# Seven up-projections and four down-projection groups, one to a slot, inside a band attention that two MLPs follow

## The chip, the cores and the metric

The kernel runs on one core of a Trainium2 chip. The metric is the device time of one execution in microseconds. A core has five engines with instruction queues of their own: TensorE (PE in the rows; PEld is its weight load), VectorE (DVE), ScalarE (ACT), GpSimd (POOL) and SyncE (SP, which here issues nearly all DMAs). They work in parallel and wait for each other through semaphores; each takes its own instructions in order.

## The reference, cut to what matters

```python
def _attn_ref(q_l, k_l, v_l, q_g, k_g, v_g):      # B=4, H=8, 512 local + 32 global rows, D=64
    s_g = scale * q_g @ k_all.T;  out_g = softmax(s_g) @ v_all         # global rows see all keys
    s_ll = where(abs(i - j) <= 32, scale * q_l @ k_l.T, -1e9)          # local rows: a band
    s_lg = scale * q_l @ k_g.T                                         # and the global keys
    out_l = softmax(concat([s_lg, s_ll])) @ concat([v_g, v_l])
    return concat([out_g, out_l], axis=2)

x = attention(...)                                 # 2304 tokens x 512
h = x @ w_in;   x = elu(h) @ w_out                 # first MLP, 512 -> 2048 -> 512
h = x2 @ w_in2; y = clipped_square(h) @ w_out2     # second MLP: ((h+1)^2/4 between -1 and 1)
```

All of it is float32.

## The kernel before, in words

**The MLPs.** The tokens stand in columns: four blocks of 512 (j = 0 to 3, one for each batch element) and one of 128 global rows (GR). An *up-projection* (class `Up`, f, j) makes 128 of the 2048 hidden features of one block: every float32 operand is split into a high and a low part, so it takes 12 matmuls of 512 columns (3 products x 4 slices), then `curve` (two ScalarE activations), `join` (VectorE), `high` (ScalarE, `gh`) and `low` (VectorE, `gl`). `down` multiplies the hidden tiles of a chunk of weights into four output tiles (d = 0 to 3), 3 matmuls for each f and d, and `collect` copies or adds the sum into `acc`. The first chunk holds f = 0 to 2, the second f = 3 to 6. The MLPs are written in plain loops, and a scheduler sets the order of the instructions on every engine; `later` puts the down matmuls three steps behind the ups.

**Weights** come as float32 pairs of words (64-bit rows, `wraw`) and are decoded by `prep` (line 160) into a high part `wh` and a low part `wl`, for a tile of 128 x 1024: an `Abs` on ScalarE, five VectorE operations, a copy to `wh` on ScalarE, and two more VectorE operations of which the last makes `wl`. In the attention a tile is decoded in two halves of 512 columns (six parts: three of up weights, then three of down weights).

**The attention** is a pipeline of 24 units, in groups of three: local rows of a pair of heads, global rows of four heads, local rows of the next pair. In slot n (the loop at line 722) unit n is at its scores (`s` or `sg`, `top`, `expo`), unit n-1 at its transposes and values (`pt` or `tg`, `po` or `pog`), unit n-2 at its norm, its transposes back (`ot`, or `tg3`, which the rows call `tg`) and the split into `xh` and `xl`. All calls inside the attention go through `Pinned`: each engine runs them in exactly the order written. Block j of the MLP is complete in x when slot 6j + 7 is through.

**Loads** stand in SP's queue in the order that `arrive` calls them: q and k of a pair, its two v halves, and the raw weight parts. `load` adds a limit: a load waits until so many older ones have landed that no more than 2700 words a partition are in flight (q 544, k 576, a v half 1040, a raw part 1024). q and k have two buffers each, v four, raw weights one.

**The dense work inside the attention** before: `early_ups` (line 672) makes five up-projections, and is stepped twice a slot from slot 10: four matmuls in the first slot of a group, eight in the second, then the curve, the join, the high and the low part each half a slot later. `early_weights` (line 665) steps a part's decode once a slot from slot 4. At the end, in slot 24, two of the four down tiles of block 0 are made (line 746). What is left of the five goes after the loop.

## Time and profile before

| | |
|---|---|
| median of 3 runs | 874.63 us (870.61 to 876.02) |
| profiled execution | 871.58 us, span 869.8 us |
| mean granted TensorE clock | 0.994 |
| busy: TensorE / VectorE / ScalarE / GpSimd | 851.5 / 584.3 / 431.2 / 47.5 us |
| attention, to the first free down matmul | 0 to 140.78 us |
| the MLPs | from there to the end |

The span is one execution as the hardware profiler saw it on the core; the time of the run beside it is longer by what lies around the span. A row of the timeline gives the start of an instruction (or of several alike in a row, "x64"), its duration, the engine, the line, the operation and its tiles, and in brackets how long the engine had idled and what ended that. Since matmuls are pipelined, the pace is read from start to start, not from the duration. Line 111 is that of `Pinned`, so every attention instruction has it and is told apart by its tile.

### The profile page before, as it was taken

To read this page: it belongs to the slowest core of one execution; us is meant where nothing else is said; L and a number is where in the kernel's file an instruction comes from. 1 tells how busy PE (TensorE), PEld (TensorE's weight loads), DVE (VectorE), ACT (ScalarE), POOL (GpSimd) and SP (SyncE) were. 2 spreads that over 40 slices of the span, in tenths; PEclk is the share of its full clock that TensorE was granted. 3 is DMA by queue.
4 is the path that set the end of the run, shared out by engine and by line. 5 is a ranking of instruction groups with operands and counts; after the bars stand their busy time and mean duration, and the time that the engine had idled before them with its cause. 6 is when DMAs were issued, how large, how long until landed. Compare 5 with 4: busy or idle time off the path is not lost.

```text
span 869.8 us, 14560 instructions
## 1 busy us (share of the span) xinstructions
PE 851.5 (98%) x5946; PEld 698.5 (80%) x5946; DVE 584.3 (67%) x1130; ACT 431.2 (50%) x755; POOL 47.5 (5%) x98
## 2 busy tenths in 40 slices
PE   8889999999999999999999999999999999999998
PEld 5666778888888888888888888888888888888886
DVE  5788874877635873833389897368859754845455
ACT  5677864766434543534256564456435433433332
POOL 4234220000000000000000000000000000000000
PEclk9999999999999999999999999999999999999999
DMA  7777751231200220110012112002201200000014
GB/s 262 252 233 232 227 174 54 101 133 55 97 1 1 96 97 1 49 49 1 1 49 96 49 50 97 0 2 98 96 0 49 97 1 1 0 1 1 2 58 148
DMA packets 19027, 65.43 MB, mean 75 GB/s; under 512 B 3984, under 2 KB 4240, under 8 KB 15248
## 3 DMA queue, kind: packets, MB, share of 16 engines
q1 hardware_dynamic: 18672, 64.23, 21.7%
q8 instruction: 47, 0.77, 0.3%
q10 hardware_dynamic: 288, 0.26, 0.1%
q14 instruction: 20, 0.16, 0.1%
HBM read 60.03 MB, written 4.46 MB: 74 GB/s over the span
## 4 chain that ended last, share of the span: by engine, by line
PE 92%; DMA 5%; ACT 1%; DVE 1%; issue 0%; POOL 0%; SPq 0%; POOLq 0%
PE dn L318 40%; PE up L245 39%; DMA v_sb<-in_vwin 4%; PE up L242 3%; PE dn L335 3%; PE s L111 2%; PE pt L111 1%; PE po L111 1%; PE up L111 1%; PE pog L111 1%; PE sg L111 1%; DMA k_sb<-in_kT 1%; ACT sn L111 1%; PE tg L111 1%; PE idle L111 1%; PE dn L111 1%
## 5 line engine op out<-in xcount | busy, mean ns | idle before, releaser
L318 PE MATMUL dn<-gh,wh 128*128 128x512 f32 x506 | 196.9, 389 | 0.0
L318 PE MATMUL dn<-gl,wh 128*128 128x512 f32 x506 | 196.8, 389 | 0.0
L318 PE MATMUL dn<-gh,wl 128*128 128x512 f32 x506 | 196.3, 390 | 0.0
L245 PE MATMUL up<-xh,wl 128*128 128x512 f32 x492 | 192.4, 391 | 0.0
L245 PE MATMUL up<-xl,wh 128*128 128x512 f32 x492 | 191.6, 390 | 0.0
L245 PE MATMUL up<-xh,wh 128*128 128x512 f32 x492 | 191.6, 389 | 0.0
L276 ACT ACTIVATE gh<-g 128x512 fp32r<-128x512 f32 x123 | 77.7, 632 | 119.1 <-DVE g L265 71.9
L295 DVE TENSOR_TENSOR acc<-dn,acc 128x512 f32<-128x512 f32 x128 | 84.8, 685 | 48.5 <-PE dn L318 48.3
L318 PEld LDWEIGHTS dn<-gl,wh 128*128 128x128 f32 x506 | 95.0, 188 | 19.8
L280 DVE TENSOR_TENSOR gl<-g,gh 128x512 fp32r<-128x512 f32 x123 | 84.6, 689 | 38.8 <-ACT gh L276 37.8
L318 PEld LDWEIGHTS dn<-gh,wh 128*128 128x128 f32 x506 | 95.0, 188 | 19.5
L318 PEld LDWEIGHTS dn<-gh,wl 128*128 128x128 f32 x506 | 95.0, 188 | 19.4
L245 PEld LDWEIGHTS up<-xh,wh 128*128 128x128 f32 x492 | 92.3, 188 | 19.2
L245 PEld LDWEIGHTS up<-xl,wh 128*128 128x128 f32 x492 | 92.4, 188 | 18.9
L245 PEld LDWEIGHTS up<-xh,wl 128*128 128x128 f32 x492 | 92.4, 188 | 18.8
L256 ACT ACTIVATE g<-up,half_sb 128x512 f32<-128x512 f32 (+1 forms) x69 | 46.9, 680 | 113.9 <-PE up L245 105.1
L264 DVE SCALAR_TENSOR_TENSOR g<-g 128x512 f32<-128x512 f32 (+1 forms) x69 | 46.9, 680 | 59.5 <-ACT g L256 59.4
L262 DVE SCALAR_TENSOR_TENSOR g<-up,g 128x512 f32<-128x512 f32 x64 | 43.4, 679 | 62.8 <-ACT g L253 62.8
L251 ACT ACTIVATE g<-up 128x512 f32<-128x512 f32 x64 | 37.8, 590 | 85.9 <-PE up L245 80.3
L265 DVE TENSOR_TENSOR g<-g,e 128x512 f32<-128x512 f32 (+1 forms) x69 | 47.0, 681 | 3.6
L178 ACT ACTIVATE top<-wraw 128x1024 f32<-128x1024 f32 x29 | 33.6, 1160 | 28.9 <-DMA wraw<-in_w 22.8
L253 ACT ACTIVATE g<-g,one_sb 128x512 f32<-128x512 f32 x64 | 45.9, 717 | 1.8
(112 smaller groups left out, 956.9 us busy)
## 6 DMA issues: line engine op xcount, KB each, us to landing
wraw<-in_w SPq DMA_DIRECT2D x29, 1024.0 KB, 4.8
v_sb<-in_vwin SPq DMA_DIRECT2D x32, 520.0 KB, 4.5
k_sb<-in_kT SPq DMA_DIRECT2D x16, 288.0 KB, 4.0
q_sb<-in_qT SPq DMA_DIRECT2D x16, 272.0 KB, 4.4
outT<-acc SPq DMA_DIRECT2D x16, 256.0 KB, 2.1
wraw<-in_w SPq DMA_DIRECT2D x6, 512.0 KB, 4.4
outT<-acc_rows SPq DMA_DIRECT2D x4, 64.0 KB, 2.2
mask_sb<-in_mask ACTq DMA_DIRECT2D x1, 192.0 KB, 4.0
```

The lines of the kernel that those rows point to most:

```text
L111: return lambda *args, **kw: tc.keep_in_program_order(fn(*args, **kw))
L245: eng.tensor.matmul(self.ps, w, x, start=k == 0, stop=k == 3 * KT - 1)
L251: eng.scalar.activation(self.g, self.ps, AF.Exp)
L253: eng.scalar.activation(self.g, self.g, AF.Relu, bias=one_sb, scale=-1.0)
L256: eng.scalar.activation(self.g, self.ps, AF.Relu, bias=half_sb, scale=0.5)
L262: eng.vector.scalar_tensor_tensor(g, self.ps, 0.0, g, ALU.max, ALU.subtract)
L264: eng.vector.scalar_tensor_tensor(g, g, 1.0, g, ALU.min, ALU.mult)
L265: eng.vector.tensor_tensor(g, g, self.e, ALU.add)
L276: eng.scalar.activation(self.gh, self.g, AF.Copy)
L280: eng.vector.tensor_tensor(self.gl, self.g, self.gh.bitcast(F32), ALU.subtract)
L295: eng.vector.tensor_tensor(a, ps, a, ALU.add)
L318: eng.tensor.matmul(banks[d], w[:, d * P:(d + 1) * P], g, start=f == fs[0] and k == 0, stop=f == fs[-1] and k == 2,)
```

## The change

- Inside the attention the tables `UPS` and `DOWNS` name what slot does what: an up-projection (f, j) with all its 12 matmuls in slots 8, 11, 14, 15, 16, 17 and 24, a down tile (j, d) of the first chunk with its 9 matmuls in slots 20 to 23. They stand behind the transposes and before the values of the slot. The curve follows in the same slot; join, high and low come in the next.
- The sums of block 0 are so complete; the two tiles made in slot 24 are of block 1. `sums` notes what the MLP's loop leaves out.
- A raw weight part is requested at the head of `arrive` in slots 3, 6, 9, 11, 13 and 15, and its decode begins two slots later: `Abs`, then a stage with `wh`, then a stage with `wl`, a slot each. Raw, `top` and `power` have two buffers in the attention.
- The decode: `wh` is rounded from the whole number, and `wl` is what that leaves plus the last bits, which come from a 16-bit word. Seven VectorE operations as before, one tensor_scalar less and one two-input operation more.
- `acc` of blocks 0 and 1 is set up before slot 20 in memory that the decode leaves; `gh` and `gl` have six buffers in place of five; the diagonal blocks for the global queries are one tile, and their zeros feed the warm-up.

```diff
-UP_EARLY = 5
 
 BANKS = (2, 3, 1)
 
-PREP_AT = 4
-UP_AT = 9
-
-UP_STEP = 4
+PREP_FROM = (3, 6, 9, 11, 13, 15)
+
+UPS = {8: (0, 0), 11: (1, 0), 14: (2, 0), 15: (0, 1), 16: (1, 1), 17: (2, 1), 24: (0, 2)}
+DOWNS = {20: (0, 0), 21: (0, 1), 22: (0, 2), 23: (0, 3)}
...
-    h_p = ctx.enter_context(tc.tile_pool(name="h", bufs=LAG + 2))
+    h_p = ctx.enter_context(tc.tile_pool(name="h", bufs=LAG + 3))
     ps_up = [ctx.enter_context(tc.tile_pool(name="ps_up", bufs=1, space=PSUM))]
     ps_dn = []
+    e_p = []
...
-    def prep(wraw_p, wtmp_p, layer, f, c0, n, raw_tag="wraw"):
+    def prep(wraw_p, wtmp_p, layer, f, c0, n, bufs=1):
...
-        raw = wraw_p.tile([P, n], U64, tag=raw_tag, name="wraw")
+        raw = wraw_p.tile([P, n], U64, tag="wraw", name="wraw", bufs=bufs)
         load(raw, (w1, w2)[layer][f][:, c0:c0 + n], 2 * n)
-        words = raw.bitcast(U32).rearrange("p (n two) -> p n two", two=2)
-        low, high = words[:, :, 0], words[:, :, 1]
-        top = wtmp_p.tile([P, n], U32, tag="top", name="top")
-        power = wtmp_p.tile([P, n], U32, tag="power", name="power")
-        rest = wtmp_p.tile([P, n], U32, tag="rest", name="rest")
+        high = raw.bitcast(U32).rearrange("p (n two) -> p n two", two=2)[:, :, 1]
+        low = raw.bitcast(U16).rearrange("p (n four) -> p n four", four=4)[:, :, 1]
         yield
 
+        top = wtmp_p.tile([P, n], U32, tag="top", name="top", bufs=bufs)
         eng.scalar.activation(top.bitcast(F32), high.bitcast(F32), AF.Abs)
-        eng.vector.tensor_scalar(rest, high, 0x1FF, 15, ALU.bitwise_and, ALU.logical_shift_left)
-        eng.vector.scalar_tensor_tensor(
-            rest, low, 17, rest, ALU.logical_shift_right, ALU.bitwise_or
-        )
         yield
-
         eng.vector.tensor_scalar(
             top.bitcast(F32), top.bitcast(F32), SMALLEST, 1.0, ALU.max, ALU.mult
         )
 
-        eng.vector.tensor_scalar(top, top, 3, 0x3FFFF000, ALU.logical_shift_left, ALU.bitwise_and)
+        eng.vector.tensor_scalar(top, top, 3, 0x3FFFFFF8, ALU.logical_shift_left, ALU.bitwise_and)
         eng.vector.scalar_tensor_tensor(
             top, high, 0xC0000000, top, ALU.bitwise_and, ALU.bitwise_or
         )
+        eng.scalar.activation(hi, top.bitcast(F32), AF.Copy)
+        power = wtmp_p.tile([P, n], U32, tag="power", name="power")
+        eng.vector.tensor_scalar(power, top, 0xFF800000, None, ALU.bitwise_and)
         yield
-        eng.scalar.activation(hi, top.bitcast(F32), AF.Copy)
-        eng.vector.tensor_scalar(power, top, 0xFF800000, None, ALU.bitwise_and)
-        eng.vector.scalar_tensor_tensor(
-            lo, rest, 2.0 ** -35, power.bitcast(F32), ALU.mult, ALU.mult
-        )
+
+        rest, number = power.bitcast(F32), top.bitcast(F32)
+        eng.vector.scalar_tensor_tensor(rest, low, 2.0 ** -36, rest, ALU.mult, ALU.mult)
+        eng.vector.tensor_tensor(number, number, hi.bitcast(F32), ALU.subtract)
+        eng.vector.tensor_tensor(lo, number, rest, ALU.add)
...
-        early = count[0] < UP_EARLY or count[0] % 4 == 0
-        count[0] += 1
+        early = len(ps_up) == 1 or count[0] % 4 == 0
+        count[0] += len(ps_up) > 1
...
-        def early_weights():
-
-            for part in parts:
-                for _ in range(3):
-                    next(part, None)
-                    yield
-
-        def early_ups():
-
-            for f, j in [(f, j) for j in range(B) for f in chunks[0][1]][:UP_EARLY]:
-                u = Up(0, f, j)
-                u.products(UP_STEP)
-                yield
-                yield
-                u.products(3 * KT - UP_STEP)
-                yield
-                u.curve()
-                yield
-                u.join()
-                yield
-                u.high()
-                yield
-                u.low()
-
-        parts = [prep(g_p, wtmp_p, 0, *part, raw_tag="wraw") for part in halves]
-        sent = iter(parts)
-        weights, ups = early_weights(), early_ups()
+        def early_down(j, d):
+
+            bank = up_bank()
+            fs = chunks[0][1]
+            for f in fs:
+                wh, wl = (w[:, KT * P:] for w in wtiles[0, f])
+                gh, gl = made[0, f, j]
+                for k, (w, g) in enumerate(((wl, gh), (wh, gh), (wh, gl))):
+                    eng.tensor.matmul(
+                        bank, w[:, d * P:(d + 1) * P], g,
+                        start=f == fs[0] and k == 0, stop=f == fs[-1] and k == 2,
+                    )
+            collect(0, fs, j, d, bank)
+            sums.add((j, d))
+
+        parts = [prep(early_wraw_p, wtmp_p, 0, *part, bufs=2) for part in halves]
+
+        def request(n):
+
+            if n in PREP_FROM:
+                next(parts[PREP_FROM.index(n)])
+
+        def prepare(n):
+
+            for i in range(4, 1, -1):
+                if n - i in PREP_FROM:
+                    next(parts[PREP_FROM.index(n - i)], None)
...
+            request(n)
...
-                next(next(sent, iter([0])))
-                if more:
...
+        u = None
         for n in range(len(units) + 2):
-            if n > UP_AT:
-                next(ups, None)
             part(n, "scores")
             part(n - 2, "norm")
+            if u:
+                u.join()
             part(n - 1, "turn")
             part(n - 1, "copy")
             part(n - 2, "back")
             part(n, "top")
             part(n - 2, "low")
             part(n, "expo")
-            if n >= PREP_AT:
-                next(weights, None)
-            if n >= UP_AT:
-                next(ups, None)
+            prepare(n)
+            if u:
+                u.high()
+                u.low()
+                u = None
+            if n in UPS:
+                u = Up(0, *UPS[n])
+                u.products(3 * KT)
+                u.curve()
+            elif n in DOWNS:
+                early_down(*DOWNS[n])
             part(n - 1, "values")
-
             arrive(n)
+            if n == min(DOWNS) - 1:
+
+                prep_ctx.close()
+                pool = mpool("acc_early", 1)
+                for j in range(2):
+                    acc[j] = pool.tile([P, KT, SL], F32, name=f"acc{j}")
             if n == len(units):
 
                 s_ctx.close()
                 ps_dn.append(mpool("ps_dn0", 1, space=PSUM))
                 for f in chunks[0][1]:
-                    down(0, chunks[0][1], 0, f, made[0, f, 0], first, range(KT // 2))
-        for _ in weights:
-            pass
-        for _ in ups:
-            pass
-        prep_ctx.close()
+                    down(0, chunks[0][1], 1, f, made[0, f, 1], first, range(KT // 2))
+                sums.update((1, d) for d in range(KT // 2))
         eng = free
 
     pool = mpool("acc", 1)
-    for j in range(1, B):
+    for j in range(2, B):
         acc[j] = pool.tile([P, KT, SL], F32, name=f"acc{j}")
     acc[GR] = pool.tile([P, KT * P], F32, name="acc_rows")
+    e_p.append(mpool("e", 1, side="right"))
...
-                    banks = {} if ci + j else first
+                    banks = first if (ci, j) == (0, 1) else {}
                 if (layer, f, j) not in made:
                     up(layer, f, j)
-                ds = range(KT) if ci + j else range(KT // 2, KT)
+                ds = [d for d in range(KT) if ci or (j, d) not in sums]
```

On **VectorE**, from the end of slot 9 (the `xl` of a global unit) to the reductions of slot 10; `den` to `o_sb` is the norm of the local unit 8. Before:

```order
L111 TENSOR_TENSOR xl_84<-tg_1111,xh_79 128x2x32
L111 TENSOR_SCALAR power<-top 128x512
L111 SCALAR_TENSOR_TENSOR wl_89<-rest,power 128x512
L111 TENSOR_SCALAR den<-po 128x8
L111 RECIPROCAL den<-den 128x8
L111 TENSOR_TENSOR o_sb<-po,den 128x2x4x64
L111 TENSOR_REDUCE m_1212<-sg 128x1 x2
```

And with the change:

```order
L112 TENSOR_TENSOR xl_84<-tg_1109,xh_79 128x2x32
L112 TENSOR_SCALAR top<-top 128x512 x2
L112 SCALAR_TENSOR_TENSOR top<-wraw,top 128x512
L112 TENSOR_SCALAR power<-top 128x512
L112 TENSOR_TENSOR gl<-g,gh 128x512
L112 TENSOR_SCALAR den<-po 128x8
L112 RECIPROCAL den<-den 128x8
L112 TENSOR_TENSOR o_sb<-po,den 128x2x4x64
L112 TENSOR_REDUCE m_1214<-sg 128x1 x2
```

The decode stage in this slot grew from two operations to four, and `gl` of the up-projection of slot 8 stands between it and the norm.

On **TensorE**, the third slot of a group (slot 11), from its scores. Before:

```order
L111 MATMUL s<-kw,q_sb 32x128 x32
L111 MATMUL tg<-eye_sb,pg 128x128 x6
L111 MATMUL ot<-eye_sb,o_sb 128x128 x4
L111 MATMUL pog<-v_sb,pgT 64x130 x12
L111 MATMUL s<-kw,q_sb 32x128 x32
L111 MATMUL pt<-eye_sb,sn 128x128 x8
```

And with the change:

```order
L112 MATMUL s<-kw,q_sb 32x128 x32
L112 MATMUL tg<-eye_sb,pg 128x128 x6
L112 MATMUL ot<-eye_sb,o_sb 128x128 x4
L112 MATMUL up<-xh_75,wl_89 128x512
L112 MATMUL up<-xl_80,wh_88 128x512
L112 MATMUL up<-xh_75,wh_88 128x512
```

Where `pog` followed `ot` at once, an up-projection stands between (nine more of its matmuls follow, then `pog`); the first slot of the next group in turn has no `up` behind its `tg`.

On **SP**, the loads of slots 11 to 13. Before:

```order
L111 DMA q_sb<-in_qT 128x544
L111 DMA k_sb<-in_kT 128x576
L111 DMA wraw<-in_w 128x512
L111 DMA v_sb<-in_vwin 128x1040 x3
L111 DMA q_sb<-in_qT 128x544
L111 DMA k_sb<-in_kT 128x576
L111 DMA v_sb<-in_vwin 128x1040
```

And with the change:

```order
L112 DMA wraw<-in_w 128x512
L112 DMA q_sb<-in_qT 128x544
L112 DMA k_sb<-in_kT 128x576
L112 DMA v_sb<-in_vwin 128x1040 x3
L112 DMA wraw<-in_w 128x512
L112 DMA q_sb<-in_qT 128x544
L112 DMA k_sb<-in_kT 128x576
L112 DMA v_sb<-in_vwin 128x1040
```

The raw part of slot 11 went ahead of q and k, and one more was put in slot 13, ahead of q, k and the second v half of pair 9.

## Rows read from the trace of the kernel before

**Rows 1.** The page, part 1: busy us (share of the span) xinstructions.

```profile
PE 851.5 (98%) x5946; PEld 698.5 (80%) x5946; DVE 584.3 (67%) x1130; ACT 431.2 (50%) x755; POOL 47.5 (5%) x98
```

**Rows 2.** Timeline of TensorE, one MLP stretch: start us, us, engine, line, operation.

```profile
146.80 0.39 PE L245 MATMUL up<-xh,wl 128*128 128x512 f32 x1
...
152.24 0.39 PE L318 MATMUL dn<-gh,wl 128*128 128x512 f32 x1
```

**Rows 3.** Timeline of TensorE in the attention: rows with long idling before them.

```profile
32.21 1.03 PE L111 MATMUL pog<-v_sb,pgT 64*64 64x130 f32 x10 [2.20 <-DMA v_sb<-in_vwin]
33.17 1.91 PE L111 MATMUL s<-kw,q_sb 64*32 64x128 f32 x64
...
44.92 0.34 PE L111 MATMUL s<-kw,q_sb 64*32 64x128 f32 x8 [1.50 <-issue]
...
80.81 1.52 PE L111 MATMUL pog<-v_sb,pgT 64*64 64x130 f32 x10 [1.32 <-DMA v_sb<-in_vwin]
...
114.28 1.03 PE L111 MATMUL pog<-v_sb,pgT 64*64 64x130 f32 x10 [1.76 <-DMA v_sb<-in_vwin]
```

**Rows 4.** Timeline of TensorE, slots 17 to 19 of the attention.

```profile
93.32 1.16 PE L111 MATMUL s<-kw,q_sb 64*32 64x128 f32 x64
...
97.53 1.16 PE L111 MATMUL s<-kw,q_sb 64*32 64x128 f32 x64
...
102.50 1.22 PE L111 MATMUL sg<-k_sb,diag 128*64 128x272 f32 x12
103.66 1.09 PE L111 MATMUL pt<-eye_sb,sn 128*128 128x128 f32 x8
...
108.55 1.45 PE L111 MATMUL s<-kw,q_sb 64*32 64x128 f32 x64
```

**Rows 5.** Windows of 1 us: busy of each engine, clock, DMA, GB/s.

```profile
116.00:117.00 1.00, 1.00 (x48) 0.74 (x32) 0.07 (x1) 0.07 (x1) 0.92 (x3) 0.50 0.86 337
```

**Rows 6.** Waits of SP's queue, 0 to 135 us: total, times, longest.

```profile
SPq L111 <- DVE top L111: 12.3, 4, 3.3
```

**Rows 7.** The page, part 6: KB each, median us to landing.

```profile
v_sb<-in_vwin SPq DMA_DIRECT2D x32, 520.0 KB, 4.5
```

**Rows 8.** Timeline of TensorE, the attention's end.

```profile
136.17 0.50 PE L111 MATMUL dn<-gh,wl 128*128 128x512 f32 x1
...
140.43 0.60 PE L111 MATMUL ot<-eye_sb,o_sb 128*128 128x128 f32 x4
140.78 0.48 PE L318 MATMUL dn<-gh,wl 128*128 128x512 f32 x1
```

**Rows 9.** Timeline of ScalarE, slots 18 and 19.

```profile
99.88 1.06 ACT L111 ACTIVATE pT<-pt 128x512 f32<-128x512 f32 x2
...
100.94 2.45 ACT L111 ACTIVATE sn<-sn,nml 128x128 f32<-128x128 f32 x8
103.28 0.62 ACT L111 ACTIVATE wh<-top 128x512 fp32r<-128x512 f32 x1
```

**Rows 10.** Timeline of VectorE, slots 18 and 19.

```profile
102.70 0.68 DVE L111 TENSOR_TENSOR gl<-g,gh 128x512 fp32r<-128x512 f32 x1
103.30 0.16 DVE L111 TENSOR_SCALAR den<-po 128x8 f32<-128x8 f32 x1
...
104.34 0.78 DVE L111 TENSOR_REDUCE m<-sg 128x1 f32<-128x272 f32 x2
```

**Rows 11.** Timeline of VectorE, weight tiles decoded in the MLP.

```profile
150.82 0.69 DVE L195 TENSOR_SCALAR power<-top 128x1024 uint32<-128x1024 uint32 x1
151.54 1.23 DVE L196 SCALAR_TENSOR_TENSOR wl<-rest,power 128x1024 fp32r<-128x1024 uint32 x1
...
183.40 1.22 DVE L196 SCALAR_TENSOR_TENSOR wl<-rest,power 128x1024 fp32r<-128x1024 uint32 x1
```

**Rows 12.** Windows of 40 us in the MLP.

```profile
460.00:500.00 40.00, 40.00 (x181) 33.08 (x180) 37.76 (x59) 24.85 (x41) 0.00 (x0) 1.00 0.18 66
```

**Rows 13.** Groups by form on VectorE, 15 to 130 us: busy, mean ns.

```profile
L111 DVE SCALAR_TENSOR_TENSOR top<-wraw,top 128x512 uint32<-128x512 uint32 x6 | 5.6, 942 | 0.2
```

More of the change, by code (lines that the diff above doesn't have):

```diff
@@ L12 @@
 F32R = mybir.dt.float32r
+U16 = mybir.dt.uint16
 U32 = mybir.dt.uint32
@@ L208, in band_attention_then_two_mlps @@
     made = {}
+    sums = set()
     def up_bank():
-        early = count[0] < UP_EARLY or count[0] % 4 == 0
-        count[0] += 1
+        early = len(ps_up) == 1 or count[0] % 4 == 0
+        count[0] += len(ps_up) > 1
         return ps_up[0 if early else 1].tile([P, SL], F32, tag="up", name="up")
@@ L254, in curve @@
             else:
-                self.e = t_p.tile([P, SL], F32, tag="e", name="e", bufs=1)[:, :self.n]
+                self.e = e_p[0].tile([P, SL], F32, tag="e", name="e")[:, :self.n]
                 eng.scalar.activation(self.g, self.ps, AF.Relu, bias=half_sb, scale=0.5)
@@ L370, in band_attention_then_two_mlps @@
     add_ring(ctx.enter_context(tc.tile_pool(name="w", bufs=1)), 0)
-    acc[0] = xpool.tile([P, KT, SL], F32, name="acc0")
     prep_ctx = ExitStack()
@@ L385, in band_attention_then_two_mlps @@
         g_p = apool("gl", 1, side="right")
+        early_wraw_p = prep_ctx.enter_context(tc.tile_pool(name="wraw0", bufs=1, side="right"))
         ps_o = apool("ps_o", BANKS[2], space=PSUM, side="right")
@@ L391, in band_attention_then_two_mlps @@
         )
-        diag = [g_p.tile([P, 64], F32, name=f"diag{i}") for i in range(4)]
+        diags = g_p.tile([P, 4, 64], F32, name="diags")
+        diag = [diags[:, i] for i in range(4)]
         def normalised(po, out):
@@ L640, in band_attention_then_two_mlps @@
         halves = [(f, c0, WCOLS // 2) for c0 in (0, WCOLS // 2) for f in range(W_EARLY)]
-        zeros = st_p.tile([P, 512], BF16, name="zeros", bufs=1)
-        eng.vector.memset(zeros, 0.0)
+        eng.vector.memset(diags, 0.0)
+        zeros = diags.rearrange("p i c -> p (i c)").bitcast(BF16)
         eng.vector.memset(half_sb, 0.5)
@@ L653, in band_attention_then_two_mlps @@
         load_v(*pairs[0])
-        for t in diag:
-            eng.vector.memset(t, 0.0)
         eng.vector.memset(nhalf_sb, -0.5)
```

## The prediction

> **What bounds the kernel now.** I read the page's busy times first: the matmul engine is busy 851.5 of 869.8 us [rows 1], so 18 us of idling is all that better cover could ever give, plus what the clock costs. Then the timeline of the engine after 140 us: from the 146.80 to the 152.24 start lie 24 matmuls of 512 columns, 0.2267 us each, with nothing between them [rows 2]. That part, the two MLPs, is bound by the matmul engine alone. So I read the attention (0 to 140.78 us), where the idling is. Its timeline shows three long waits in the middle of a global unit's value matmuls (`pog`), of 2.20, 1.32 and 1.76 us, each for a `v_sb` transfer, and one of 1.50 us that the profile cannot explain ("issue") [rows 3]. After the wait that ends at 32.21 the next score matmuls take 1.91 us [rows 3], while undisturbed ones take 1.16 [rows 4]: in the stretch from 116 to 117 us, behind the wait that ends at 114.28, the granted clock is 0.50, the 1.2 GHz level [rows 5]. Such a fall costs about 1.5 us, since transposes slow down likewise. Last I read the issuing queue: SP stood 12.3 us waiting for VectorE to let go of the one raw weight buffer [rows 6], with the v loads queued behind it; a v load lands 4.5 us after issue [rows 7].
>
> **What moves, and its worth.** 12 matmuls for each of two more up-projections and 36 for four down groups go from the MLP into the attention; the two half-groups at its end stay, for block 1 in place of block 0. After the attention 42 matmuls fewer remain: 42 x 0.2267 = 9.5 us off [rows 2]. Inside the attention a dense piece costs 0.2367 us a matmul: 18 from 136.17 to 140.43 take 4.26 [rows 8], so 2.84 for an up-projection and 2.13 for a down group. What matters is whether they fill waits or lengthen slots.
>
> A group of three slots (local, global, local) without projections and waits takes the engine about 11.7 us: 4.21 for the last slot, from 93.32 to 97.53, and for the two before it the 11.02 from 97.53 to 108.55, less 12 projection matmuls (2.84) and 0.7 of short waits [rows 4].
>
> **Where pieces sit in every slot (groups 5 and 7),** the matmul engine sets the time: 11.7 + 3 x 2.84 = 20.2, and 11.7 + 3 x 2.13 = 18.1. The tail after the last `pog` (eight transposes, an up-projection, the last values, 18 down matmuls) comes to 9.8, much as now.
>
> **Where one piece sits in the third slot alone (groups 3, 4, 6),** the first two slots hold 3.5 + 3.6 us of matmuls but the whole chain from projection to weights. I walk it from the start of the first slot's scores. ScalarE can copy `pT` from about 1.6 us (scores and four transposes), 1.06 long, then an `xh` of 0.1, then the eight exponentials, 2.34 from 100.94 to 103.28, which ends them at 5.15; then `wh` and `gh`, some 0.55 each [rows 9], to 6.25. VectorE has been done with its decode since 4.8, but `gl`, which needs `gh`, stands in its queue ahead of the norm of the next slot. `gl` ends at 6.85 (0.60 from 102.70 to 103.30) and the norm, 1.04 long, at 7.9 [rows 10]. TensorE reaches the `ot` transposes, which need that norm, at 5.6: **a wait of 2.3 us**, and the values matmuls are queued behind it. After that norm come the global unit's two reductions, 0.78 [rows 10], a 0.2 us `nm` and its exponentials, some 0.9, to 9.75; the third slot's scores need their PSUM and so wait a little, and with `tg` they last to 11.55. The second `ot` waits 0.9 more for VectorE, which has a 0.6 us `xl`, three two-input decode operations (0.6 each) and another norm to do, to 12.45. `ot`, the up-projection and `pog` (the last slot's 4.21 less scores and `tg` is 2.4) end the group at 17.5; group 6, with a down group instead, at 16.8. Group 2 has no `gl` pending and loses the later waits alone, 0.35 and 0.9: 11.7 + 2.84 + 1.25 = 15.8. Today `gh` runs ahead of `pT` and nothing of this waits; the 12 matmuls are spread over the first two slots, which is the cover that goes.
>
> **The loads.** With two raw buffers SP's wait for VectorE disappears in most slots, and the piece ahead of `pog` gives v time to land, so the waits of rows 3 go in groups 3, 6 and 7. In group 4 it is the reverse: the raw part requested in slot 13 needs part two's buffer, whose last reader runs about 10.2 us into the group, and the second v load is queued behind it and, by the limit on words in flight, behind its landing: 10.2 + 4.5 + 4.5 = 19.2 [rows 7], against a second half of `pog` that could start at 16.9. I take 2.0 us of wait there (bounds 0 and 2.5). Early on, a raw load leaves the queue ahead of `v_sb` of pair 2, worth 0.7 us at the first `pog` wait (bounds 0 and 2.2); the half-rate stretch behind it stays, 1.6.
>
> **The decode** swaps one tensor_scalar for a two-input operation: 1.23 against 0.69 at 1,024 columns, +0.54 a tile [rows 11]. In the MLP it is hidden: VectorE is at its fullest 37.76 of 40 us between 460 and 500 [rows 12], and two or three tiles fall into such a stretch, 1.6 us. If that cover were gone it would cost those 1.6 us a chunk change. In the attention it lies in the walk.
>
> A `top` operation with two inputs, raw words and `top`, takes 0.942 us on average in the attention [rows 13], against 0.68 for `gl` of the same size [rows 10]: something there holds it up. The Trainium skill (SBUF — State Buffer, "Who interferes with whom") says that a VectorE instruction with two SBUF inputs and a GpSimd instruction that reads SBUF block each other. That speaks against the change, since a decoded part now has four such operations in place of three. By that rule one more of them for each of six parts is 6 x 0.26 = 1.6 us more of VectorE, and the sum would be 877.7 in place of the one below.
>
> **The sum.** From the scores of slot 6 to the first free matmul: 15.8 + 17.5 + (17.5 + 2.0) + 20.2 + 16.8 + 18.1 + 9.8 + 1.6 = 119.3. Now it is 140.78 - 33.17 = 107.6 [rows 3, 8]. So +11.7 there, -0.7 before it, -9.5 behind it: **+1.5 us**. The profiled execution took 871.58 us, so 873.1 against it; the median shown is 874.63, 3.05 above, and my time for the median is **876.1**.
>
> **Rivals.**
> A. The cover works: VectorE keeps ahead and every group is bound by matmuls. Then the stretch is 6 x 11.7 + 6 x 2.84 + 4 x 2.13 + 9.8 + 1.6 = 107.1, that is -0.5 - 0.7 - 9.5 = -10.7: 863.9. For it: no `pog` wait is left without a piece ahead of it. Against it: it needs `gl` not to hold the norm. Halfway lies 870.
> B. The clock (slower). Four waits of 2 us or more (slots 10, 13, 14 and 19) are as long as those behind which the rows show 0.50 [rows 3, 5]; with 1.5 us lost behind each, +6: 882.1, and with the rest of the waits a little longer 885. It decides from a wait of about 1.3 us, the shortest with a fall; the 1.50 us one at 44.92 had none, so it is not sure. The Trainium skill (TensorE: Matmul & The Clock Gate, "What's actually happening") has the reduced rate as the default that activity releases; the trace agrees in the direction, with falls behind idling alone.
> C. The MLP's second chunk finds its weights late. The fourth tile is ready at 183.40 + 1.22 = 184.6 [rows 11], 43.8 us after the attention, 46.0 with four slower decodes; its first matmul comes some 232 matmuls, 52.6 us, into that part. Spare 6.6 us; if each tile slips 3 us, +5.4: 881.5.
>
> **How the numbers follow.** My forecast has 0.51 and alone reaches from 871 to 881; A has 0.22, B 0.22, C 0.05. About 1% of this kernel, 8.7 us, is what can be told from no change: under 865.9 or over 883.4. Of A somewhat more than half lies below that line: 0.13 faster. Of B 0.10, of C 0.02 and of the forecast 0.02 lie above: 0.14 slower. The range is 866 to 885, from most of the way to A up to B's end.
>
> **What would show it.** First free down matmul near 152 us (A: near 140, B: near 158). `ot` waiting for `o_sb` or `den` of VectorE in slots 10, 13 and 19, about 2 us each; a `pog` wait in slot 14 and in no other of groups 3 to 7. SP waiting for the raw buffer twice or less. No matmul idling between 160 us and the end. I am wrong if `ot` does not wait: then the norm is early, and A holds; or if the granted clock falls in each group.

## The result, and the profile after

The changed kernel takes **877.64 us** (median of 14 runs, 875.42 to 879.13) against 871.62 for the kernel before (14 runs beside them): a ratio of **1.0059 [1.0046, 1.0073]**, which makes it 5.1 us slower (the two medians differ by 6.0). The profiled executions are 875.42 and 871.58 us, with spans of 873.6 and 869.8.

The page's busy times of the changed kernel, the line that answers to [rows 1]:

```profile
PE 851.1 (97%) x5946; PEld 697.2 (80%) x5946; DVE 599.2 (69%) x1126; ACT 430.1 (49%) x755; POOL 48.1 (6%) x98
```

TensorE is as busy as before, 851.1 against 851.5, so the 3.8 us of added span are idling. Its timeline has the first free down matmul at 155.40, where it was at 140.78 [rows 8]:

```profile
155.40 0.48 PE L316 MATMUL dn<-gh,wl 128*128 128x512 f32 x1
```

The attention is thus 14.6 us longer, and what follows is 873.6 - 155.40 = 718.2 against 729.0 us, 10.8 shorter. A window from 12 us to that first free matmul splits the 14.6 (columns as in [rows 5]: length, busy time of TensorE, its weight loads, VectorE, ScalarE, GpSimd, then clock, DMA share, GB/s). Before:

```profile
12.00:140.78 128.78, 116.86 (x2556) 91.62 (x2551) 95.22 (x408) 88.19 (x233) 42.52 (x84) 0.96 0.65 209
```

After:

```profile
12.00:155.40 143.40, 127.25 (x2569) 98.48 (x2551) 97.09 (x409) 93.57 (x241) 43.20 (x84) 0.98 0.59 192
```

TensorE is busy 10.4 us longer there and idle 143.40 - 127.25 = 16.15 us, where it idled 11.92. So the pieces that moved in are paid in full in the attention, which alone would leave the time as it was, and 4.2 us of idling came on top. The waits of TensorE from 12 to 155 us, by what ended them (total, times, longest), name it:

```profile
PE ot L112 <- DVE o_sb L112: 11.0, 7, 2.9
PE pog L112 <- DMA v_sb<-in_vwin: 2.8, 3, 2.0
PE s L112 <- issue: 1.5, 3, 1.0
```

Of the three waits for `v_sb` of [rows 3] the first is nearly as long as before (2.00 us), the second is down to 0.58 and the third is gone; waits of `ot` for VectorE's norm have taken their place. The timeline of TensorE shows the three long ones, in slots 10, 13 and 19, and what is left of the wait for v in slot 14 (87.55):

```profile
58.45 0.82 PE L112 MATMUL ot<-eye_sb,o_sb 128*128 128x128 f32 x4 [2.49 <-DVE o_sb L112]
59.20 1.96 PE L112 MATMUL po<-v_sb,pT 128*32 128x65 f32 x64
...
77.31 0.63 PE L112 MATMUL ot<-eye_sb,o_sb 128*128 128x128 f32 x4 [2.49 <-DVE o_sb L112]
77.87 1.11 PE L112 MATMUL po<-v_sb,pT 128*32 128x65 f32 x64
...
87.55 1.03 PE L112 MATMUL pog<-v_sb,pgT 64*64 64x130 f32 x10 [0.58 <-DMA v_sb<-in_vwin]
...
118.02 0.63 PE L112 MATMUL ot<-eye_sb,o_sb 128*128 128x128 f32 x4 [2.86 <-DVE o_sb L112]
```

Behind the first, `po` took 1.96 us, behind the second 1.11: only the first was followed by a low clock. Windows of 5 us around them say the same in the clock column (the last figure but two):

```profile
60.00:65.00 5.00, 4.54 (x121) 3.86 (x114) 4.90 (x22) 1.90 (x5) 3.05 (x5) 0.78 0.70 196
75.00:80.00 5.00, 2.62 (x114) 2.12 (x119) 3.96 (x10) 3.30 (x7) 0.00 (x0) 1.00 0.10 37
```

How the first wait comes about stands on VectorE's timeline in slots 9 and 10:

```profile
53.38 0.88 DVE L112 TENSOR_SCALAR top<-top 128x512 f32<-128x512 f32 x2
...
55.01 0.43 DVE L112 TENSOR_SCALAR power<-top 128x512 uint32<-128x512 uint32 x1
56.58 0.69 DVE L112 TENSOR_TENSOR gl<-g,gh 128x512 fp32r<-128x512 f32 x1 [1.14 <-ACT gh L112]
57.19 0.16 DVE L112 TENSOR_SCALAR den<-po 128x8 f32<-128x8 f32 x1
...
57.62 0.69 DVE L112 TENSOR_TENSOR o_sb<-po,den 128x512 f32<-128x512 f32 x1
```

and on ScalarE's:

```profile
53.06 2.44 ACT L112 ACTIVATE sn<-sn,nml 128x128 f32<-128x128 f32 x8
55.40 0.63 ACT L112 ACTIVATE wh<-top 128x512 fp32r<-128x512 f32 x1
55.92 0.62 ACT L112 ACTIVATE gh<-g 128x512 fp32r<-128x512 f32 x1
```

VectorE has finished the decode at 55.4 and then stands 1.14 us for `gh`, which waits on ScalarE behind eight exponentials and `wh`. The norm (`den`, its reciprocal, `o_sb`), whose input is ready, stands in VectorE's queue behind `gl`, and TensorE behind the norm.

SP's waits, against [rows 6]: SP waits for VectorE to let go of a raw buffer twice, in place of four times, and 7.3 us in place of 12.3.

```profile
SPq L112 <- DVE power L112: 7.3, 2, 7.1
```

### The profile page after: what moved, and what is told of

The parts are those of the page before. It is cut to its first block, busy times and chain, and to the rows that moved or that the text cites. A ratio compares the mean times of both kernels' runs of the same rounds, so it can differ in the third digit from the quotient of the medians.

```text
span 873.6 us, 14558 instructions
## 1 busy us (share of the span) xinstructions
PE 851.1 (97%) x5946; PEld 697.2 (80%) x5946; DVE 599.2 (69%) x1126; ACT 430.1 (49%) x755; POOL 48.1 (6%) x98
## 4 chain that ended last, share of the span: by engine, by line
PE 90%; DVE 4%; DMA 3%; ACT 2%; issue 0%; SPq 0%
PE dn L316 39%; PE up L243 38%; PE up L240 3%; PE dn L333 2%; PE up L112 2%; DMA v_sb<-in_vwin 2%; PE pog L112 1%; PE s L112 1%; PE pt L112 1%; DVE top L112 1%; PE po L112 1%; PE ot L112 1%; DMA k_sb<-in_kT 1%; DVE o_sb L112 1%; ACT sn L112 1%; ACT pT L112 0%
## 5 line engine op out<-in xcount | busy, mean ns | idle before, releaser
L316 PE MATMUL dn<-gh,wh 128*128 128x512 f32 x494 | 192.4, 390 | 0.0
L316 PE MATMUL dn<-gh,wl 128*128 128x512 f32 x494 | 192.0, 390 | 0.0
L316 PE MATMUL dn<-gl,wh 128*128 128x512 f32 x494 | 191.3, 389 | 0.0
L243 PE MATMUL up<-xh,wl 128*128 128x512 f32 x484 | 189.2, 391 | 0.0
L243 PE MATMUL up<-xl,wh 128*128 128x512 f32 x484 | 188.5, 390 | 0.0
L243 PE MATMUL up<-xh,wh 128*128 128x512 f32 x484 | 188.4, 390 | 0.0
L316 PEld LDWEIGHTS dn<-gl,wh 128*128 128x128 f32 x494 | 92.8, 188 | 19.3
L243 PEld LDWEIGHTS up<-xl,wh 128*128 128x128 f32 x484 | 90.9, 188 | 18.5
L249 ACT ACTIVATE g<-up 128x512 f32<-128x512 f32 (+2 forms) x62 | 36.6, 591 | 100.2 <-PE up L243 95.8
L260 DVE SCALAR_TENSOR_TENSOR g<-up,g 128x512 f32<-128x512 f32 (+2 forms) x62 | 41.9, 677 | 45.1 <-ACT g L251 45.1
L255 ACT ACTIVATE e<-up,nhalf_sb 128x512 f32<-128x512 f32 (+1 forms) x69 | 46.5, 674 | 2.0 <-DVE g L263 2.0
```

The lines of the kernel that those rows point to most:

```text
L243: eng.tensor.matmul(self.ps, w, x, start=k == 0, stop=k == 3 * KT - 1)
L249: eng.scalar.activation(self.g, self.ps, AF.Exp)
L255: eng.scalar.activation(self.e, self.ps, AF.Relu, bias=nhalf_sb, scale=0.5)
L260: eng.vector.scalar_tensor_tensor(g, self.ps, 0.0, g, ALU.max, ALU.subtract)
L316: eng.tensor.matmul(banks[d], w[:, d * P:(d + 1) * P], g, start=f == fs[0] and k == 0, stop=f == fs[-1] and k == 2,)
```

## The experiments

**gl behind the next norm.** The two halves of a piece's hidden layer are made apart: `gh` where it was, `gl` after the norm of the next slot.

```
             part(n - 2, "norm")
+            if split:
+                split.low()
+                split = None
...
                 u.high()
-                u.low()
-                u = None
+                split, u = u, None
```

> The changed kernel with gl of an up-projection moved one place: it is made after the norm of the next slot, in place of ahead of it. Theory (gl, which waits for gh on ScalarE, holds the norm, and so the ot transposes and all behind them): ot waits in slots 10, 13 and 19 fall from 2.49, 2.49 and 2.86 us to 0.3 to 0.8 each, no half rate behind slot 10; 6 us less than the changed kernel, 871 to 872, ratio to the kernel before 0.998 to 1.001. Rival (VectorE simply has too much to do in these slots, in whatever order): ot waits stay above 1.8, ratio 1.004 to 1.007.

Measured: 1.0011 [0.9995, 1.0028], first free down matmul at 151.95. The waits in slots 10, 13 and 19 are 0.66, 0.66 and 1.26 us, the last more than was expected, as is the ratio by a little. On VectorE in slot 10 the order is turned round, and nothing stands idle:

```profile
56.09 0.43 DVE L112 TENSOR_SCALAR power<-top 128x512 uint32<-128x512 uint32 x1
...
56.86 0.69 DVE L112 TENSOR_TENSOR o_sb<-po,den 128x512 f32<-128x512 f32 x1
57.65 0.69 DVE L112 TENSOR_TENSOR gl<-g,gh 128x512 fp32r<-128x512 f32 x1
```

That `gl`, where it stood, holds the norm is shown by this. By the difference of the two ratios it costs 4.2 us, about 2 to 6 with their intervals, the low clock behind slot 10 included (the clock there is 1.00 in this run). It is not the only cause: see the old decode's operations below.

**gh right behind the join**, the other way to bring `gl` forward: ScalarE makes `gh` ahead of the exponentials.

```
             if u:
                 u.join()
+                u.high()
             part(n - 1, "turn")
 ...
             if u:
-                u.high()
                 u.low()
```

> The changed kernel with gh made right behind join, ahead of the exponentials on ScalarE; gl keeps its place on VectorE. Theory: VectorE no longer idles 1.1 us for gh, the norm still stands behind the decode and gl, so ot waits of about 1.0 to 1.4 us are left in slots 10, 13 and 19: 3 to 4.5 us less than the changed kernel, ratio 1.001 to 1.003. Rival (too much VectorE work): no change, ratio 1.005 to 1.007.

Measured: 1.0050 [1.0033, 1.0066], a miss: the ratio is the rival's, though its condition fails, since the three `ot` waits are 1.25 us each, as expected. The groups behind group 2 are only 1.9 us shorter together, since waits of 1.3 to 1.6 us come up in slots 11, 18 and 20. And in the profiled execution, the slowest of nine (879.46 us), group 2 took 22.1 us in place of 17.6: in slot 8 the scores waited 3.21 us for nothing the profile shows, and the clock fell behind it. TensorE's row, and the window of 5 us around it, whose clock is 0.61:

```profile
47.19 1.11 PE L112 MATMUL s<-kw,q_sb 64*32 64x128 f32 x32 [3.21 <-issue]
```

```profile
45.00:50.00 5.00, 2.81 (x41) 2.42 (x41) 2.75 (x19) 0.62 (x2) 2.49 (x5) 0.61 0.47 138
```

Such a wait in slot 8 has the kernel before too, 1.50 us [rows 3]; the changed kernel's profile has none there. The last section comes back to it.

**The new decode alone**, in the kernel before with its one raw buffer.

```
         yield
-        eng.scalar.activation(hi, top.bitcast(F32), AF.Copy)
-        eng.vector.tensor_scalar(power, top, 0xFF800000, None, ALU.bitwise_and)
-        eng.vector.scalar_tensor_tensor(
-            lo, rest, 2.0 ** -35, power.bitcast(F32), ALU.mult, ALU.mult
-        )
+
+        rest, number = power.bitcast(F32), top.bitcast(F32)
+        eng.vector.scalar_tensor_tensor(rest, low, 2.0 ** -36, rest, ALU.mult, ALU.mult)
+        eng.vector.tensor_tensor(number, number, hi.bitcast(F32), ALU.subtract)
+        eng.vector.tensor_tensor(lo, number, rest, ALU.add)
```

> The kernel before with the new decode operations alone, still one stage a slot and with one raw buffer. Theory: the decode lies beside other work, +0 to +1 us, ratio 0.999 to 1.0015, matmul engine without idling in the MLPs. Rival (the added two-input operation costs VectorE and GpSimd time that decides, in the attention or at the changes of chunk): half of the loss or more, ratio 1.003 to 1.006.

Measured: 1.0257 [1.0234, 1.0280], which neither theory allowed: the slowest kernel of all. The waits of TensorE, then SP's:

```profile
PE po L112 <- DMA v_sb<-in_vwin: 14.0, 8, 3.0
PE pog L112 <- DMA v_sb<-in_vwin: 9.2, 6, 2.8
```

```profile
SPq L112 <- DVE power L112: 37.6, 5, 9.0
```

The new decode's last reading of the raw words comes a slot later (`power<-wraw,power`). SP stood 37.6 us in front of the one raw buffer, where it stood 12.3 [rows 6], with v's loads behind it.

**The same with two raw buffers.**

```
-        raw = wraw_p.tile([P, n], U64, tag=raw_tag, name="wraw")
+        raw = wraw_p.tile([P, n], U64, tag=raw_tag, name="wraw", bufs=bufs)
...
-        parts = [prep(g_p, wtmp_p, 0, *part, raw_tag="wraw") for part in halves]
+        parts = [prep(g_p, wtmp_p, 0, *part, raw_tag="wraw", bufs=2) for part in halves]
```

> The kernel before with the new decode, and with two buffers for the raw words in the attention where the run with the decode alone had one. Theory: that run's 22 us came from the one raw buffer, which the last multiplication now holds a slot longer, with v's loads queued behind the next raw load; with two buffers the waits of po and pog for v_sb fall from 23.2 us to about the 7 us of the kernel before, and the decode's extra VectorE work hides: ratio to before 0.998 to 1.003, first free down matmul at 140 to 143 us. Rival: VectorE's extra work, 0.54 us a tile in the attention and in the MLP, is what costs, or the pace of the tiles in the MLP: ratio still 1.015 or more, with waits of PE on DVE tiles.

Measured: 0.9997 [0.9976, 1.0018], first free down matmul at 141.31. The two lines on v fall from 23.2 to 6.6 us:

```profile
PE pog L112 <- DMA v_sb<-in_vwin: 4.1, 2, 2.5
...
PE po L112 <- DMA v_sb<-in_vwin: 2.5, 2, 1.3
```

So in the schedule of the kernel before the decode's arithmetic costs nothing that can be told, within some 2 us, in the attention or in the MLP; its longer hold of the one raw buffer does, and the change's second buffer takes that away. In the changed schedule its operations do cost something, as the run with the old ones shows below.

**No pieces named for the attention.** The tables are empty, and 138 matmuls go back to the MLP's loops, the two half-groups at the attention's end among them.

```
-UPS = {8: (0, 0), 11: (1, 0), 14: (2, 0), 15: (0, 1), 16: (1, 1), 17: (2, 1), 24: (0, 2)}
-DOWNS = {20: (0, 0), 21: (0, 1), 22: (0, 2), 23: (0, 3)}
+UPS = {}
+DOWNS = {}
...
```

> The changed kernel with no up-projection and no down group inside the attention (none of slots 8 to 24, and not the two tiles of slot 24); all of them are made in the MLP, 138 matmuls or 31.3 us more there. Theory: inside, the pieces lengthen the attention by most of what they weigh, so without them it ends near 155.4 - 32.7 - 7 (ot waits) + 7 (waits for v that come back) = 121 to 127, and the whole takes 870 to 876, ratio 0.998 to 1.005. Rival (the pieces hide in waits of the attention and are worth their weight): it ends at 135 or later, ratio above 1.012.

Measured: 1.0135 [1.0108, 1.0163], with the first free down matmul at 135.78: as the rival said, and not the theory. But the run is no clean price of the pieces. The scheduler put 24 up-projection matmuls of the MLP's line 243 (from 46.80 us on) and six down matmuls into the attention by itself, and the attention's last `ot` starts at 141.07, behind that first down matmul; in the changed kernel it starts at 155.04. So 108 matmuls fewer shorten the attention by 14.0 us. And with more idling the clock is lower, here in groups 5 and 6 (0.89 and 0.80, where the changed kernel has 1.00 and 1.00):

```profile
87.30:104.80 17.50, 13.90 (x328) 10.60 (x326) 14.95 (x57) 11.29 (x30) 6.58 (x11) 0.89 0.71 220
104.80:122.00 17.20, 15.00 (x334) 11.49 (x334) 12.92 (x54) 10.04 (x28) 8.14 (x18) 0.80 0.63 195
```

**The old decode's operations in the attention**, with the new schedule (the MLP keeps the new ones). `wh` and `power` move a slot on, out of the way of `gh` and `gl`.

```
+        if bufs == 2:
...
+            eng.vector.scalar_tensor_tensor(
+                top, high, 0xC0000000, top, ALU.bitwise_and, ALU.bitwise_or
+            )
+            yield
+            eng.scalar.activation(hi, top.bitcast(F32), AF.Copy)
+            eng.vector.tensor_scalar(power, top, 0xFF800000, None, ALU.bitwise_and)
+            eng.vector.scalar_tensor_tensor(
+                lo, rest, 2.0 ** -35, power.bitcast(F32), ALU.mult, ALU.mult
+            )
+            return
```

> The changed kernel with the old decode's operations for the six parts in the attention (the MLP keeps the new ones): wh and power move out of the slot in which gh and gl of a piece are made. Theory (the second o_sb wait is ACT's and DVE's work ahead of the norm): gh starts at the end of the exponentials, so gl and o_sb come 0.5 us earlier in slots 10, 13 and 19: the three ot waits 1.9 to 2.0, 1.9 to 2.0 and 2.3 in place of 2.49, 2.49 and 2.86; the kernel gains about 1.5 us, ratio to before 1.003 to 1.006. Rival (the new decode's operations are what slows the attention, by more VectorE work and more waits on it): groups 2 to 5 fall back by 1 us or more each, ratio 1.000 to 1.002.

Measured: 0.9997 [0.9979, 1.0015]. Two of the three waits are to the digit what the theory gave, on TensorE's timeline in slots 10 and 13:

```profile
58.40 1.00 PE L112 MATMUL ot<-eye_sb,o_sb 128*128 128x128 f32 x4 [1.97 <-DVE o_sb L112]
...
76.15 0.63 PE L112 MATMUL ot<-eye_sb,o_sb 128*128 128x128 f32 x4 [1.98 <-DVE o_sb L112]
```

but the gain of some 5 us is more than the 1.5 that was expected of them, and the ratio is the rival's: groups 2, 3 and 4 are 1.0 to 1.2 us shorter, as it said, and group 5 is 0.3. The wait in slot 19 is 1.56, and of the smaller ones in slots 7, 8, 11 and 17 (2.5 us together) and the 1.02 of "issue" in slot 20 none over 0.3 us is left, though slot 14's grew from 1.08 to 1.41 and slot 20 has a new one of 0.72. In slots 7 and 8 no piece has a `gl` pending, so the waits there were the decode's own. The new decode's operations thus cost some 5 us in the changed schedule, with `gl` where it stood, and each of the two edits by itself takes about the whole loss away: both stand ahead of the same norm. Which of the moved operations does it was not tried apart.

**The pieces in the first slot of a group**, in place of the third.

```
-UPS = {8: (0, 0), 11: (1, 0), 14: (2, 0), 15: (0, 1), 16: (1, 1), 17: (2, 1), 24: (0, 2)}
+UPS = {9: (0, 0), 12: (1, 0), 15: (2, 0), 16: (0, 1), 17: (1, 1), 18: (2, 1), 24: (0, 2)}
```

> The changed kernel with the six up-projections of slots 8, 11, 14, 15, 16, 17 in slots 9, 12, 15, 16, 17, 18. Theory (PE waits in the second slot of a group because gl, made in the slot behind a piece, holds the norm there): the piece's gh and gl now fall in slots 10, 13 and 16, ahead of the norm of the slot after, so the waits of ot in slots 10, 13 and 19 of 2.5 to 2.9 us become at most 1.0, and a wait of about 1 to 2 us comes up in slots 11, 14 and 17 in its place, on ot or on v_sb: ratio 1.001 to 1.006. Rival (the sum of PE's work and not the place of the waits sets the stretch): all waits of ot together fall by 5 us and nothing comes in their place, ratio 0.998 to 1.000.

Measured: 1.0104 [1.0081, 1.0126], slower than either theory allowed. The waits moved as expected: none in slots 10, 13 and 19, but these on TensorE in slots 11 and 14:

```profile
64.99 1.11 PE L112 MATMUL ot<-eye_sb,o_sb 128*128 128x128 f32 x4 [1.91 <-DVE nml L112]
66.02 3.26 PE L112 MATMUL pog<-v_sb,pgT 96*64 96x130 f32 x24
...
89.14 1.76 PE L112 MATMUL pog<-v_sb,pgT 64*64 64x130 f32 x10 [2.03 <-DMA v_sb<-in_vwin]
```

What had not been expected is the clock behind both (0.50 is 1.2 GHz), with `pog` at 3.26 us where 24 of its matmuls take 1.85 elsewhere:

```profile
65.00:70.00 5.00, 5.00 (x60) 3.66 (x68) 2.57 (x18) 3.49 (x10) 1.45 (x4) 0.50 0.73 225
...
90.00:95.00 5.00, 5.00 (x82) 3.66 (x80) 2.40 (x19) 0.88 (x2) 3.56 (x10) 0.50 0.70 220
```

**v ahead of the raw words**, on top of `gl` late: a slot's raw request goes behind its other loads, and the first moves from slot 3 to slot 4.

```
-PREP_FROM = (3, 6, 9, 11, 13, 15)
+PREP_FROM = (4, 6, 9, 11, 13, 15)
 ...
         def arrive(n):
-            request(n)
 ...
             arrive(n)
+            request(n)
```

> The version with gl behind the next norm, and the raw words requested behind a slot's other loads, the first of them in slot 4 in place of 3. Theory (what is left to take is the waits of pog for v_sb in slots 5 and 14, 2.78 and 0.71 us there, since a raw load stands ahead of v's in SP's queue): these fall to 1.0 and 0.3 or less, ratio to before 0.997 to 1.000. Rival (the loads are bound by their sum in this stretch, 0.8 of the DMA engines' time, whatever their order): the wait in slot 5 stays within 0.5 us of 2.78 or moves to a wait of up for wl in slot 8, ratio 1.000 to 1.003.

Measured: 1.0023 [1.0007, 1.0039]. The waits for v fell as the theory said (0.96 us in slot 5, none in slot 14), but the weights of the first piece come late, the second outcome that the rival allowed, and the clock is down behind it:

```profile
47.72 0.79 PE L112 MATMUL up<-xh,wl 128*128 128x512 f32 x1 [4.19 <-DVE wl L112]
```

**The raw words last, all in their slots** (without the first line of that edit).

> The version with gl behind the next norm, and the raw words requested behind a slot's other loads, all in the slots of the change (the first in slot 3). Theory (in the run with the first request in slot 4 groups 4 and 6 were 1.1 and 1.3 us shorter, and only the wait of up for wl in slot 8, 4.19 us, took it back): that wait is gone, the pog wait in slot 14 stays at 0.3 or less, the one in slot 5 comes back to 2 to 3 us; ratio to before 0.9975 to 1.0000. Rival (the groups' gain there was the late start of part 1 and not the order): as with gl late alone, 1.0000 to 1.0020.

Measured: 1.0006 [0.9984, 1.0027]: no gain that can be told from `gl` late alone, as the rival said. The profiled execution has 2.92 us of "issue" in slot 8, which by itself would hide one.

**Two edits, and all three.** First `gl` late with the old decode:

> Two edits that each took about 4 us on their own, together: gl behind the next norm, and the old decode's operations for the six parts in the attention. Theory (both shorten what stands on DVE and ACT ahead of the norm in the slot behind a piece): they share most of it; the ot waits of slots 10, 13 and 19 stay at the 0.66 to 1.3 of the first edit, and what the old decode takes besides (0.8 to 1.0 us in groups 2 and 6) adds 1 to 3 us: ratio to before 0.9975 to 1.0000. Rival (the two take the same 4 us, and the stretch is then bound by PE's work): 1.0000 to 1.0020.

Measured: 0.9979 [0.9956, 1.0003], as expected. Then with the raw words last as well:

> All three edits together: gl behind the next norm, the old decode's operations in the attention, and the raw words requested last. If the gains of the pairs add: first free down matmul at 147 to 150 us, ratio to before 0.9950 to 0.9985. Rival (PE's own work, 27 us of pieces in the attention, bounds groups 5 and 7 whatever waits are taken away): 0.9985 to 1.0010.

Measured: **0.9966 [0.9942, 0.9991]**, 869.07 us against 873.19 for the kernel before beside it, first free down matmul at 146.97: faster than both kernels. The window that was shown of both above, and its waits:

```profile
12.00:146.97 134.97, 126.17 (x2597) 98.72 (x2590) 94.22 (x411) 93.55 (x241) 41.93 (x84) 0.97 0.63 205
```

```profile
PE pog L112 <- DMA v_sb<-in_vwin: 3.8, 3, 2.3
PE ot L112 <- DVE o_sb L112: 2.8, 5, 1.1
```

TensorE does nearly the work of the changed kernel there (126.17 against 127.25) and idles 8.8 us in place of 16.15. That is 3.1 under the kernel before: what the pieces bring once little of theirs is in the way. What the raw words last add to the pair before can't be told, since the two intervals overlap.

**All three without the down groups.**

```
-DOWNS = {20: (0, 0), 21: (0, 1), 22: (0, 2), 23: (0, 3)}
+DOWNS = {}
```

> The kernel with all three edits, without the four down-projection groups in slots 20 to 23: their 36 matmuls (8.2 us at 0.2267 us) stand in the MLP again. Theory (in slots 21 to 23 PE has no idle time, so three of the four stand there at full price; only the one in slot 20 fills waits): groups 6 and 7 get shorter by 6 to 8 us and the MLP longer by 8.2, so the time is 0 to 2 us above the one with all three edits. Rival (down groups fill waits of PE on DVE): 4 to 8 us above it.

Measured: 0.9965 [0.9941, 0.9989], 869.56 us. Groups 6 and 7 with the tail are 42.8 - 37.1 = 5.7 us shorter and the MLP 8.1 longer, which makes 2.4 us in the profiled executions; the medians differ by 0.5, within the theory's 0 to 2, and the two ratios can't be told apart. What there was to fill is read from this kernel, without the groups: its group 6, then slot 21 to the end of the attention.

```profile
104.00:118.80 14.80, 12.43 (x330) 9.33 (x326) 13.79 (x56) 10.45 (x27) 6.50 (x12) 1.00 0.68 222
118.80:141.20 22.40, 22.36 (x439) 17.59 (x437) 11.22 (x55) 14.04 (x39) 2.78 (x6) 1.00 0.40 131
```

22.36 busy of 22.40: three of the four groups stand where nothing was to be filled. The one in slot 20 lengthens group 6 by 0.45 us alone (15.24 with it, 14.79 without), so most of it fills idling.

## Why the prediction was right, and where it was not

**The sign and the mechanism: right.** A difference within 1% was forecast, with three waits of `ot` behind VectorE's norm, and they came in slots 10, 13 and 19 (2.49, 2.49, 2.86 for "about 2 each"). The walk through slot 9 put the end of the exponentials at 5.15 us after the slot's first scores, the norm's end at 7.9; measured from the scores at 50.21 these are 5.2 and 8.1 us. Putting `gl` behind the norm, with the decode as it was, took most of the loss away, so its place is a cause. That the old decode's operations took away as much shows that it is not the only one: the walk has the decode and `wh` on the way to that norm too, but the prediction gave them no price of their own.

**The number: partly luck.** The sum was +1.5 us; the profiled executions differ by 3.8 and the medians by 6.0. The forecast of 876.1 came that near to 877.64 because it stood on a median of three runs, 874.63, where 14 runs give 871.62: on that footing it would have been 873.1. Two slips in the sum run against each other as well. The walk's last step, 12.45 + 2.4 + 2.84, is 17.7 and not 17.5 (17.0 in group 6), 0.6 us over three groups; and the MLP's term, below, is 1.4 too small. Without them the sum is 11.7 + 0.6 - 0.7 - 10.9 = +0.7 us.

**By terms**, from the scores of slot 6 to the first free matmul, 119.3 forecast, 122.7 measured:

| term | forecast | measured |
|---|---|---|
| change ahead of it | -0.7 | -0.5 |
| group 2, with the half rate | 15.8 + 1.6 | 17.55 |
| group 3 | 17.5 | 18.86 |
| group 4, with the wait for v | 17.5 + 2.0 | 19.44 |
| group 5 | 20.2 | 20.52 |
| group 6 | 16.8 | 18.71 |
| group 7 | 18.1 | 17.8 |
| tail | 9.8 | 9.87 |
| change after it | -9.5 | -10.8 |

Groups 3 and 6 are the terms that were mis-sized. In group 3 the wait is 0.2 longer and the clock fell behind it: from `ot` to the next `tg` (58.45 to 62.62) it took 4.17 us, where the same work in slots 13 and 14 (77.31 to 80.45) took 3.14 at 2.4 GHz. In group 6 it is 2.86 in place of 2.3, with 1.02 of "issue" behind it. Group 4 is right as a sum and wrong in its parts: the wait for v was 0.58 us, not 2.0. The second half of `pog` could start 17.9 us into the group, not 16.9, behind waits of 2.49 and 1.08, and v was there at 18.5, not 19.2.

**The MLP's term was miscounted.** 42 matmuls were taken off; the groups of instructions behind the first free down matmul say 48. Of the three lines each (with the same count) one stands, before and then after:

```profile
L318 PE MATMUL dn<-gh,wh 128*128 128x512 f32 x506 | 196.9, 389 | 0.0
...
L245 PE MATMUL up<-xh,wl 128*128 128x512 f32 x488 | 190.8, 391 | 0.0
```

```profile
L316 PE MATMUL dn<-gh,wh 128*128 128x512 f32 x494 | 192.4, 390 | 0.0
...
L243 PE MATMUL up<-xh,wl 128*128 128x512 f32 x484 | 189.2, 391 | 0.0
```

3 x 12 + 3 x 4 = 48, by 0.2267 = 10.9: the 60 that moved, less the 12 of one up-projection that the kernel before already did ahead of its first free down matmul.

**The decode** was costed at nothing in the MLP, and the run with two raw buffers bears that out; with one buffer it would have cost 22 us, a hold that the prediction didn't price (the change has two buffers). For the attention it was left to the walk, without a price: there the old operations took some 5 us off, which overlap with what `gl` costs. VectorE in the window of [rows 12] is fuller, 38.59 of 40 us, and TensorE has no idling:

```profile
460.00:500.00 40.00, 40.00 (x186) 33.25 (x186) 38.59 (x58) 24.77 (x40) 0.00 (x0) 1.00 0.15 53
```

**VectorE beside GpSimd.** In one place where GpSimd makes a band of keys two-input operations of VectorE took 1.3 us in place of 0.69, and GpSimd's four operations 3.83 us, where four such take 2.37 at 69.88 us; in another, at 61.9 us, `wl` took 0.69 and GpSimd's four 2.88. VectorE's rows, then GpSimd's:

```profile
107.04 1.32 DVE L112 TENSOR_TENSOR top<-top,wh 128x512 f32<-128x512 f32 x1
...
109.08 1.30 DVE L112 TENSOR_TENSOR gl<-g,gh 128x512 fp32r<-128x512 f32 x1
```

```profile
106.82 3.83 POOL L112 TENSOR_SCALAR kw<-k_sb 128x768 f32<-128x768 f32 x4 [0.95 <-DMA k_sb<-in_kT]
```

But these lie in group 5, where TensorE was busy 20.04 of 20.5 us, so no cost of them can be seen. The rule of the Trainium skill (SBUF — State Buffer, "Who interferes with whom"), that such operations of the two engines block each other, agrees with these rows in kind. That the sum by this rule was 877.7 is chance: the operation it was read from, `top<-wraw,top`, fell from 0.942 [rows 13] to 0.692 us on average.

**The rivals.** A (the pieces fill) fails by the idle time, 16.15 us. B (the clock) came behind one of the three long waits, not all, and cost 1.0 us there, not 1.5. C (late weights) is out: TensorE has no wait behind 155.40 us, and is busy 705.00 of the 705 us from 155 to 860.

**Where the gain went.** 48 matmuls in the attention are 11.4 us of TensorE's time (0.2367 each) and save 10.8 behind it. They can gain only by filling idle time, of which 12 us were there; in the change the idling grew to 16, with 11.0 us of waits for the norm, 7.8 of them in the three slots where both `gl` and the decode stand ahead of it.

## What to carry to other kernels

Moving work into a stretch pays by the idle time it fills there, and not by its own length: count the engine's idling in the window before and after, slot by slot, and put nothing where the engine is full. Ask of each moved piece what it leaves in the in-order queues behind it: one operation that waits for another engine, ahead of work that is ready, cost some 4 us here, and letting it stand behind that work gave them back. Where two edits each take a whole loss away, as `gl` late and the old decode did, both stood on one path, and their gains add only in part (0.9979 together). And an operation that reads a load's buffer one stage later holds it longer: that cost 22 us here with one buffer, and nothing that could be told with two.

## What was not expected of the hardware

The clock does not follow the length of a wait alone. It fell to 1.2 GHz behind waits of 2.49 us (slot 10 of the changed kernel), of 1.97 (the same slot with the old decode), of 1.91 and of 1.69 with 2.03 (pieces in the first slot), and stayed at 2.4 behind 2.49 and 2.86 us in slots 13 and 19 of the changed kernel and behind 1.98 in slot 13 with the old decode. None of the runs tells what decides.

The wait of the scores without a releaser ("issue"), in the middle of a slot's 64 score matmuls, was 0 to 3.2 us in slot 8 of kernels that differ little; it took back gain of two edits in their profiled executions. Its end goes with something else in the traces. The profile has a DMA queue of the kind "instruction", 47 packets and 0.77 MB in the changed kernel. The ten such waits of over 0.6 us in slots 8 and 20 of all kernels here end 2.3 to 2.9 us after a packet of that queue moved: at 42.4 us for the wait that ends at 44.92 before, at 44.7 for 47.19 with `gh` early, at 44.4 for 46.98 with the raw words last, at 119.5 for 121.77 in slot 20 of the changed kernel. In slot 8 of the changed kernel, without such a wait, the packet moved at 39.6, before the scores began. That TensorE stands there for its own instructions is the likely reading; it is not shown, since no run moved these packets.
